# Loading both token halves of the first chunk ahead of its weights, and transposing them in one go ahead of all products

## The chip, the cores and the metric

The kernel runs on one core of a Trainium2 chip. The metric is the device time of one execution in microseconds (us). "Span" is the time from the first to the last instruction in a trace; it is about 1.9 us shorter than the device time.

## The reference

Two independent attention blocks, A and B, whose outputs are put side by side. Each projects 512 tokens of width 1024 to 32 query heads, attends to a cache with 4 key/value heads, and projects back.

```python
B, Sq, D = 16, 32, 1024              # 16*32 = 512 tokens
Hq, Hkv, Sk, Dh = 32, 4, 512, 128
q = (x @ wq).reshape(B, Sq, Hq, Dh).transpose(0, 2, 1, 3)
k, v = repeat(k_cache, 8, axis=1), repeat(v_cache, 8, axis=1)
p = softmax(einsum("bhqd,bhkd->bhqk", q, k) * Dh ** -0.5)
o = einsum("bhqk,bhkd->bhqd", p, v)
out = o.transpose(0, 2, 1, 3).reshape(B, Sq, Hq * Dh) @ wo    # bf16; for A and for B
```

## The kernel before

Only the first 8 us matter here. `x` has 1024 columns, which are 8 chunks of 128. Chunk `d` of `x`, transposed, is multiplied with chunk `d` of `wq`, and the products of the 8 chunks accumulate in PSUM, the on-chip memory that takes TensorE's results (SBUF is the one that holds its operands). The first 8 heads are computed chunk by chunk, so that TensorE can begin when the first pieces land. `TT` is 4 (128 tokens each), `NF` is 6, `HC` is 4.

```python
# loads, issued by SyncE in this order
load_x(0, 0, TT // 2)             # x columns of chunks 0 and 1, tokens 0..255, 128 KB
load_w0(0, 1, 0, NF // 2)         # weight chunk 0, heads 0..2, 96 KB
load_x(0, TT // 2, TT)            # tokens 256..511, 128 KB
load_w0(0, 1, NF // 2, NF)        # weight chunk 0, heads 3..5, 96 KB
load_w0(1, 2, 0, NF)              # weight chunk 1, heads 0..5, 192 KB
load_x(2, 0, TT)                  # chunks 2 and 3, all tokens, 256 KB
load_w0(2, 3, 0, NF)
load_w0(3, 4, 0, NF)
# ... cut: more loads

def warm_up(n):                   # products of constants, to wake TensorE's clock
    for _ in range(n):
        nc.tensor.matmul(first_q[HALF][:, 0:P], lhsT=warm, rhs=warm, start=True, stop=True)

# transpose_x(d, t0, t1, copy, ps): one TensorE transpose per 128 tokens, then one copy PSUM -> SBUF
# first_heads(heads, dcs, t0, t1): the products of these heads, chunks and tokens

warm_up(22)
for tt in range(2):
    transpose_x(0, tt, tt + 1, nc.vector.tensor_copy)
transpose_x(1, 0, 2, nc.scalar.copy, spare)
warm_up(2)
first_heads((0, 1, 2), (0,), 0, 1)
transpose_x(0, 2, TT, nc.vector.tensor_copy)
transpose_x(1, 2, TT, nc.scalar.copy)
first_heads((0, 1, 2), (0,), 1, 2)
warm_up(1)
first_heads((0, 1, 2), (0,), 2, TT)
first_heads((3, 4, 5), (0,), 0, 2)
first_heads((3, 4, 5), (0,), 2, TT)
first_heads(range(0, NF - 2), (1,))      # from here on: weight chunk 1
transpose_x(2, 0, TT, nc.vector.tensor_copy)
transpose_x(3, 0, TT, nc.scalar.copy)
first_heads(range(NF - 2, NF), (1,))
# ... cut: chunks 2 to 7, then projections, scores and values interleaved to the end
```

Of the kernel before, what the change touches and what calls it, by code (L numbers as in the profile page):

```python
# [8 lines left out]
BF16 = mybir.dt.bfloat16  # L9
# [7 lines left out]
P = 128  # L17
# [5 lines left out]
HALF = REP // 2  # L23
# [158 lines left out]
def kernel(  # L182
# [14 lines left out]
    nc = tc.nc  # L197
    B, SQ, D = A_x.shape
    SK = A_k_cache.shape[2]
    NTOK = B * SQ  # L200
    DC = D // P
    KC = SK // P
    TT = NTOK // P
# [14 lines left out]
    def fast_path(ok_i):  # L218
        with ExitStack() as fctx:
# [6 lines left out]
            psum = enter(tc.tile_pool(name="psum", bufs=2, space=bass.MemoryType.PSUM))  # L226
            enter(tc.manual_schedule())

            warm = nc.const_aps.tensor(1.0, [P, P], BF16)
# [225 lines left out]
            NF = REP - 2  # L455
# [8 lines left out]
            def load_x(d0, t0, t1):  # L464
                nc.sync.dma_start(
                    out=x_sb[:, t0:t1, d0 * P:(d0 + 2) * P],
                    in_=x_v[:, t0:t1, d0 * P:(d0 + 2) * P],
                )
# [7 lines left out]
            def load_w0(d0, d1, h0, h1):  # L476
                nc.sync.dma_start(
                    out=w0[d0 // HC][:, d0 % HC:(d1 - 1) % HC + 1, h0 * DH:h1 * DH],
                    in_=wq_v[:, d0:d1, h0 * DH:h1 * DH],
                )  # L480

            nc.scalar.preload_act_table_set("natural_log_exp_and_others")
            load_x(0, 0, TT // 2)
            load_w0(0, 1, 0, NF // 2)
            load_x(0, TT // 2, TT)
            load_w0(0, 1, NF // 2, NF)
            load_w0(1, 2, 0, NF)
            load_x(2, 0, TT)
# [18 lines left out]
            first_q = []  # L507
            for _ in range(2):
                pair_ps = psum.tile([P, 2, NW], FP32, name="q_ps", tag="s")
                first_q += [pair_ps[:, k, :] for k in range(2)]  # L510
            spare = psum.tile([P, NTOK], BF16, name="xT_ps", tag="proj")
            first_q += [psum.tile([P, NW], FP32, name="q_ps", tag="proj")[:] for _ in range(2)]

            def warm_up(n):
                for _ in range(n):
                    nc.tensor.matmul(  # L516
                        first_q[HALF][:, 0:P], lhsT=warm, rhs=warm, start=True, stop=True
                    )

            def transpose_x(d, t0, t1, copy, ps=None):  # L520
                if ps is None:
                    ps = psum.tile([P, NTOK], BF16, name="xT_ps", tag="ob")
                for tt in range(t0, t1):
                    nc.tensor.transpose(  # L524
                        ps[:, tt * P:(tt + 1) * P], x_sb[:, tt, d * P:(d + 1) * P], ident[:]
                    )
                ts = slice(t0 * P, t1 * P)
                copy(out=xT[0][:, d, ts], in_=ps[:, ts])

            def first_heads(heads, dcs, t0=0, t1=TT):  # L530
                ts = slice(t0 * P, t1 * P)
                for dc in dcs:
                    for h in heads:
                        nc.tensor.matmul(  # L534
                            first_q[h][:, ts],
                            lhsT=w0[dc // HC][:, dc % HC, h * DH:(h + 1) * DH],
                            rhs=xT[0][:, dc, ts],
                            start=(dc == 0 and t0 == 0),
                            stop=(dc == DC - 1),
                        )  # L540

            warm_up(22)
            for tt in range(2):
                transpose_x(0, tt, tt + 1, nc.vector.tensor_copy)
            transpose_x(1, 0, 2, nc.scalar.copy, spare)
            warm_up(2)
            first_heads((0, 1, 2), (0,), 0, 1)
            transpose_x(0, 2, TT, nc.vector.tensor_copy)
            transpose_x(1, 2, TT, nc.scalar.copy)
            first_heads((0, 1, 2), (0,), 1, 2)  # L550
            warm_up(1)
            first_heads((0, 1, 2), (0,), 2, TT)
            first_heads((3, 4, 5), (0,), 0, 2)
            first_heads((3, 4, 5), (0,), 2, TT)
            first_heads(range(0, NF - 2), (1,))
            transpose_x(2, 0, TT, nc.vector.tensor_copy)
            transpose_x(3, 0, TT, nc.scalar.copy)
# [68 lines left out]
            for i in range(total_slots + LAG):  # L626
                live = i < total_slots
                k, o = divmod(i, GRP)
# [52 lines left out]
    ok_i = flag.tile([1, 1], I32, name="ok_i")  # L681
    total = 2 * 2 * NG * QW
    ok = fast_path(ok_i)
    with tc.If(ok < total, preferred_fallthrough_block=True, label="general"):
        general_path(tc, problems, out_flat)
# [30 lines left out]
```

## Time and profile before

| | before |
|---|---|
| device time, median of the first 3 runs | 343.72 us (343.41 to 344.13) |
| span of the profiled run | 341.47 us |
| TensorE busy | 337.4 us, 99% of the span |
| first product of weight chunk 1 | 6.15 us |
| span minus that start | 335.32 us |

In the profile's lines, PE is TensorE, PEld its weight loads, DVE VectorE, ACT ScalarE, and SPq SyncE issuing loads. L516 is the warm-up matmul, L524 the transpose, L534 the products of the first heads, L301 the later projections. A matmul of 128x256 has 256 columns of the moving operand.

First the page of the kernel before: the span, the first line of busy time, and the chain of waits.

```profile
span 341.5 us, 5512 instructions
...
PE 337.4 (99%) x2130; PEld 214.4 (63%) x2130; DVE 265.6 (78%) x337; ACT 185.8 (54%) x209; POOL 46.7 (14%) x206
...
PE 99%; ACT 0%; issue 0%; ACTq 0%
```

TensorE bounds the kernel. But busy time covers each matmul's latency, and matmuls overlap (the page gives a 512-column one a mean of 379 ns, while they start 216 ns apart), so 99% does not prove that it runs densely. For that I compared start times. From 6.15 us to the end, 512-column matmuls start every 215 or 216 ns, and no start is late by more than 25 ns. The total is thus one number, the start of the chunk-1 products, plus a fixed train.

Next, the timeline of TensorE in the kernel before around that start. Columns: start, length, engine, line, operation, operands, shape, count.

```profile
3.24 0.63 PE L524 MATMUL xT_ps<-ident,x_sb 128*128 128x128 bf16 x4
3.67 0.42 PE L516 MATMUL q_ps<-const-bfloat16-1.0 128*128 128x128 bf16 x2
3.88 0.53 PE L534 MATMUL q_ps<-xT,w_sb 128*128 128x128 bf16 x3
4.20 0.63 PE L524 MATMUL xT_ps<-ident,x_sb 128*128 128x128 bf16 x4
4.63 0.46 PE L534 MATMUL q_ps<-xT,w_sb 128*128 128x128 bf16 x3
4.93 0.22 PE L516 MATMUL q_ps<-const-bfloat16-1.0 128*128 128x128 bf16 x1
5.00 2.19 PE L534 MATMUL q_ps<-xT,w_sb 128*128 128x256 bf16 x13
```

The last line merges the 9 remaining products of chunk 0 with the first 4 of chunk 1, as if there were no gap. The weight loads of the same stretch show the gap (the bracket is idle time of this unit and what ended it):

```profile
4.93 0.94 PEld L534 LDWEIGHTS <-w_sb 128*128 128x128 bf16 x9
6.15 0.55 PEld L534 LDWEIGHTS <-w_sb 128*128 128x128 bf16 x4 [0.28 <-DMA w_sb<-in_A_wq_dram]
```

The chain of waits of the kernel before, in order of time (start, length, what), misses it as well, because the modelled end of the matmul before it fills the hole:

```profile
5.14 1.00 PE q_ps L534 x9
6.15 0.00 issue
6.15 1.04 PE q_ps L534 x4
```

The start times say more. The last chunk-0 product starts at 5.87 and takes up 109 ns, so the next could start at 5.98. It starts at 6.15, just after weight chunk 1 landed at 6.10. Of the gap, 0.17 us is real idle time, ended by a transfer.

### The profile page before, as it was taken

The numbers are of one execution on the slowest core, as the hardware profiler recorded it, in microseconds if no ns is written. First come the engines' busy times: TensorE is split into PE (matmuls) and PEld (weight loads), VectorE is DVE, ScalarE is ACT, GpSimd is POOL, SyncE is SP. The second block draws the span as 40 slices with busy tenths as digits, with TensorE's granted clock in tenths as the row PEclk, the third lists the DMA queues.
The fourth block names the chain that finished last, engine by engine and source line by source line (L and its number), as shares of the span: only waits on it lengthen the run. The fifth ranks groups of instructions, "written<-read, shape, count | busy, mean of one in ns | idle before, by whom it ended". The sixth has DMA issues, their size and how long they took to land.

```text
span 341.5 us, 5512 instructions
## 1 busy us (share of the span) xinstructions
PE 337.4 (99%) x2130; PEld 214.4 (63%) x2130; DVE 265.6 (78%) x337; ACT 185.8 (54%) x209; POOL 46.7 (14%) x206
## 2 busy tenths in 40 slices
PE   8999999999999999999999999999999999999996
PEld 7455666666666666666666666666666666666555
DVE  1046988888988898888888988879888888889540
ACT  3058666666667667666645545555555555555110
POOL 0001110011111111110012221222122101111100
PEclk9999999999999999999999999999999999999999
DMA  6999999989996987999999955998649998440001
GB/s 194 300 192 262 295 264 196 238 244 267 277 247 154 232 232 223 192 313 263 316 272 290 280 148 142 334 270 239 117 109 291 354 186 180 98 113 6 18 18 33
DMA packets 128094, 71.70 MB, mean 210 GB/s; under 512 B 75840, under 2 KB 127296, under 8 KB 128064
## 3 DMA queue, kind: packets, MB, share of 16 engines
q1 hardware_dynamic: 127536, 70.21, 84.3%
q0 software_dynamic: 384, 1.05, 0.8%
q8 instruction: 17, 0.28, 0.3%
q14 instruction: 13, 0.11, 0.1%
q10 hardware_dynamic: 144, 0.07, 0.1%
HBM read 50.86 MB, written 2.10 MB: 155 GB/s over the span
## 4 chain that ended last, share of the span: by engine, by line
PE 99%; ACT 0%; issue 0%; ACTq 0%
PE f_ps L320 32%; PE q_ps L301 28%; PE ob L425 16%; PE s_ps L357 16%; PE q_ps L534 4%; PE q_ps L516 1%; PE xT_ps L524 0%; ACT o_sb L329 0%; ACTq L329 0%
## 5 line engine op out<-in xcount | busy, mean ns | idle before, releaser
L365 ACT ACTIVATE p_sb<-s_ps,shift 128x1024 bf16<-128x1024 f32 x128 | 142.6, 1114 | 97.7 <-PE s_ps L357 85.1
L376 DVE TRANSPOSE_TENSOR_REDUCE parts<-p_sb 128x32 f32<-128x1024 bf16 x128 | 158.7, 1240 | 20.9 <-ACT p_sb L365 19.3
L320 PE MATMUL f_ps<-wo_sb,oT 128*128 128x512 bf16 (+1 forms) x544 | 132.3, 366 | 0.0
L301 PE MATMUL q_ps<-xT,wq_sb 128*128 128x512 bf16 x448 | 116.9, 379 | 0.0
L425 PE MATMUL ob<-p_sb,v_sb 128*128 128x256 bf16 x512 | 76.8, 273 | 0.0
L357 PE MATMUL s_ps<-qT,kT 128*128 128x256 bf16 x512 | 76.8, 273 | 0.0
L320 PEld LDWEIGHTS <-oT 128*128 128x128 bf16 x544 | 53.2, 98 | 35.3
L357 PEld LDWEIGHTS <-kT 128*128 128x128 bf16 x512 | 56.9, 113 | 28.3
L301 PEld LDWEIGHTS <-wq_sb 128*128 128x128 bf16 x448 | 43.8, 98 | 32.2
L425 PEld LDWEIGHTS <-v_sb 128*128 128x128 bf16 x512 | 50.1, 98 | 20.0
L447 DVE TENSOR_TENSOR oT<-r,ob 128x512 bf16<-128x512 f32 x64 | 43.9, 686 | 20.0 <-PE ob L425 19.4
L411 DVE STREAM_TRANSPOSE r<-rall 128x512 f32<-128x512 f32 x64 | 44.2, 691 | 1.1
L309 ACT CAST qT<-q_ps 128x512 bf16<-128x512 f32 x56 | 32.6, 583 | 16.6 <-PE q_ps L301 16.6
L394 POOL COPY half<-cs 64x32 f32<-64x32 f32 x32 | 6.5, 204 | 232.1 <-DVE cs L384 232.0
L329 ACT CAST o_sb<-f_ps 128x512 bf16<-128x512 f32 (+1 forms) x17 | 9.5, 558 | 23.6 <-PE f_ps L320 23.6
L534 PE MATMUL q_ps<-xT,w_sb 128*128 128x512 bf16 (+2 forms) x73 | 14.9, 359 | 0.0
L384 DVE TENSOR_REDUCE cs<-parts 128x32 f32<-128x128 f32 x32 | 12.0, 376 | 1.1
L406 DVE RECIPROCAL rall<-sums 128x32 f32<-128x32 f32 x32 | 10.2, 319 | 3.3 <-POOL sums L403 3.3
L534 PEld LDWEIGHTS <-w_sb 128*128 128x128 bf16 x73 | 7.1, 102 | 6.8 <-DMA w_sb<-in_A_wq_dram 0.3
L566 DVE CAST qT<-q_ps 128x512 bf16<-128x512 f32 x4 | 2.5, 683 | 10.2 <-PE q_ps L534 10.2
L331 POOL DMA_DIRECT2D out_dram<-o_sb x8 | 4.6, 574 | 29.3 <-ACT o_sb L329 29.3
L395 POOL TENSOR_TENSOR half<-half,cs 64x32 f32<-64x32 f32 x32 | 7.8, 243 | 2.6
(25 smaller groups left out, 46.1 us busy)
## 6 DMA issues: line engine op xcount, KB each, us to landing
v_sb<-in_A_v_cache_dram SPq DMA_DIRECT2D x16, 512.0 KB, 5.7
wq_sb<-in_B_wq_dram SPq DMA_DIRECT2D x8, 1024.0 KB, 5.7
wo_sb<-in_A_wo_dram SPq DMA_DIRECT2D x8, 1024.0 KB, 7.1
v_sb<-in_B_v_cache_dram SPq DMA_DIRECT2D x16, 512.0 KB, 4.6
wo_sb<-in_B_wo_dram SPq DMA_DIRECT2D x8, 1024.0 KB, 8.1
wq_sb<-in_A_wq_dram SPq DMA_DIRECT2D x5, 1024.0 KB, 5.9
wq_sb<-in_A_wq_dram SPq DMA_DIRECT2D x2, 512.0 KB, 7.3
kT<-in_A_k_cache_dram SPq DMA_TRANSPOSE x64, 4.4
```

The source lines that it names most:

```text
L301: nc.tensor.matmul(ps[:], lhsT=w[:, dc, (h % 4) * DH:(h % 4 + 1) * DH], rhs=xT[pr][:, dc, :], start=(dc == 0), stop=(dc == DC - 1),)
L309: nc.scalar.copy(out=qT[pr, g][:, :, hl, :], in_=ps[:].rearrange("p (b s) -> p b s", s=SQ),)
L320: nc.tensor.matmul(ps[:, 0:width], lhsT=oT[pr, tt][:, h, :], rhs=wo_tiles[pr, nh, h // REP][:, h % REP, off:off + width], start=(h == 0), ...
L357: nc.tensor.matmul(s_ps[:, c, :], lhsT=kT[:, i % GRP, c, :], rhs=qT[pr, g][:, b, :, :].rearrange("p h s -> p (h s)"), start=True, stop=True,)
L365: nc.scalar.activation(out=p_sb[:], in_=s_ps[:], func=ACTF.Exp, bias=shift[:], scale=SCALE)
L376: nc.vector.tensor_reduce(out=parts[k][:, q, :, :].rearrange("p c h -> p (c h)"), in_=st[i]["p"][:].rearrange("p c (h s) -> p (c h) s", s=SQ),
L384: nc.vector.tensor_reduce(out=cs[:], in_=parts.pop(k)[:].rearrange("p q c h -> p q h c"), axis=AX.X, op=ALU.add,)
L406: nc.vector.reciprocal(out=rall[:, k, :], in_=quad.pop(k)[:])
L411: nc.vector.transpose(out=r[:].rearrange("p n s -> p (n s)"), in_=rall[:, k, o * 2 * REP:(o + 1) * 2 * REP] .unsqueeze(2).to_broadcast([P, ...
L425: nc.tensor.matmul(ob[j][:, q, :], lhsT=v_sb[:, i % GRP, c, :], rhs=st[i]["p"][:, c, :], start=(c == 0), stop=(c == KC - 1),)
L447: nc.vector.tensor_tensor(out=out, in0=rcp.pop(j)[:].rearrange("p (q h) s -> p q h s", h=REP), in1=ob.pop(j)[:].rearrange("p q (h s) -> p ...
L534: nc.tensor.matmul(first_q[h][:, ts], lhsT=w0[dc // HC][:, dc % HC, h * DH:(h + 1) * DH], rhs=xT[0][:, dc, ts], start=(dc == 0 and t0 == 0 ...
```

## The change

The intent was a smoother start: get both token halves of `x` on chip first, transpose all 8 blocks in a row, and then run all products of chunk 0 with no transpose between them. Three filler warm-ups go, and heads 3 to 5 run at 512 columns instead of twice 256. The second spare PSUM tile takes the buffers in which heads 4 and 5 later accumulate, so the warm-ups had to aim at head 3.

```diff
--- before.py
+++ after.py
@@ -481,8 +481,8 @@
 
             nc.scalar.preload_act_table_set("natural_log_exp_and_others")
             load_x(0, 0, TT // 2)
+            load_x(0, TT // 2, TT)
             load_w0(0, 1, 0, NF // 2)
-            load_x(0, TT // 2, TT)
             load_w0(0, 1, NF // 2, NF)
             load_w0(1, 2, 0, NF)
             load_x(2, 0, TT)
@@ -508,13 +508,13 @@
             for _ in range(2):
                 pair_ps = psum.tile([P, 2, NW], FP32, name="q_ps", tag="s")
                 first_q += [pair_ps[:, k, :] for k in range(2)]
-            spare = psum.tile([P, NTOK], BF16, name="xT_ps", tag="proj")
+            spare = [psum.tile([P, NTOK], BF16, name="xT_ps", tag="proj") for _ in range(2)]
             first_q += [psum.tile([P, NW], FP32, name="q_ps", tag="proj")[:] for _ in range(2)]
 
             def warm_up(n):
                 for _ in range(n):
                     nc.tensor.matmul(
-                        first_q[HALF][:, 0:P], lhsT=warm, rhs=warm, start=True, stop=True
+                        first_q[NF // 2][:, 0:P], lhsT=warm, rhs=warm, start=True, stop=True
                     )
 
             def transpose_x(d, t0, t1, copy, ps=None):
@@ -540,18 +540,12 @@
                         )
 
             warm_up(22)
-            for tt in range(2):
-                transpose_x(0, tt, tt + 1, nc.vector.tensor_copy)
-            transpose_x(1, 0, 2, nc.scalar.copy, spare)
-            warm_up(2)
-            first_heads((0, 1, 2), (0,), 0, 1)
-            transpose_x(0, 2, TT, nc.vector.tensor_copy)
-            transpose_x(1, 2, TT, nc.scalar.copy)
-            first_heads((0, 1, 2), (0,), 1, 2)
-            warm_up(1)
-            first_heads((0, 1, 2), (0,), 2, TT)
-            first_heads((3, 4, 5), (0,), 0, 2)
-            first_heads((3, 4, 5), (0,), 2, TT)
+            for k, ts in enumerate(((0, TT // 2), (TT // 2, TT))):
+                transpose_x(0, *ts, nc.vector.tensor_copy)
+                transpose_x(1, *ts, nc.scalar.copy, spare[k])
+            for ts in ((0, TT // 2), (TT // 2, TT)):
+                first_heads(range(0, NF // 2), (0,), *ts)
+            first_heads(range(NF // 2, NF), (0,))
             first_heads(range(0, NF - 2), (1,))
             transpose_x(2, 0, TT, nc.vector.tensor_copy)
             transpose_x(3, 0, TT, nc.scalar.copy)
```

## The prediction

> **What bounds the kernel now.** TensorE. The page gives PE 337.4 us busy of a span of 341.5, and the chain of waits is 99% PE. By the start-to-start times of the matmuls in the trace, from 6.15 us on, no start is late by more than 25 ns (one, at 7.93, waits for a VectorE copy): 512-column products start every 216 ns to the end. The total is therefore "when the products of weight chunk 1 start" plus a fixed train of about 335 us. Only what moves 6.15 pays.
>
> The first 6.15 us, from the timeline: 22 warm-ups (0.93 to 3.24, one per 107 ns), then transposes, 3 more warm-ups and the chunk-0 products without a gap, the last of them starting at 5.87. The next could start at 5.98, but starts at 6.15, released by the landing of weight chunk 1 at 6.10. The clock releases in the middle: 128-column matmuls start every 107 ns until about 4.85 us, then 512-column ones every 216. The Trainium skill, "TensorE: Matmul & The Clock Gate", section "Wait — 56ns, not 53.3ns?", gives 107/427 ns cold and 56/216 ns warm for 128/512 columns; the trace agrees (107, 216; 256 columns warm took 109).
>
> **What the change does.**
> - Loads: the second x half moves from third to second place, the first weight half from second to third. Issues are about 0.5 us apart, landings 2.2 to 2.3 us after issue: estimated x halves 3.0 and 3.5 us (was 4.04), first weights 4.0 to 4.1 (was 3.41). The second weight half (4.78), chunk 1 (6.10) and everything later have the same bytes ahead of them and the same place in the queue, so should land as before.
> - PE: removes 3 warm-ups (about 0.3 us, two cold). Eight transposes run together from 3.24 to about 4.1. Then heads 0-2 on 256 columns twice, instead of 128, 128, 256 columns: the same columns. Heads 3-5 at 512 columns: 3 matmuls instead of 6.
> - Copies: three VectorE copies become two (0.29 us each for 256 columns); two ScalarE copies (0.37 us) stay. All end in time.
>
> Estimated PE line: transposes to 4.1, heads 0-2 first half cold (3 x 213 ns) to 4.75, second half, partly warm, to 5.15, heads 3-5 (3 x 216) to 5.8. PE then waits for chunk 1, landing at 6.10.
>
> **On the critical path:** nearly nothing. About 0.2 us less PE work before 6.15 becomes idle time (0.17 to about 0.35 us) in front of the same landing. From there the same instructions run. If in some executions the clock releases later, that PE work would have passed 6.10 and removing warm-ups saves up to 0.3 us; a chunk 1 landing moved by the reorder could add or take 0.2.
>
> **Prediction:** 343.6 us, 8 in 10 within 342.9 to 344.4. Faster by over 2%: 0.005; within 2%: 0.99; slower by over 2%: 0.005.
>
> **What would show each step.** Second x half landing near 3.5 and first weights near 4.05; first product at 4.1 instead of 3.88; last chunk-0 product ending about 5.8; first chunk-1 product still at 6.1 to 6.2, released by a DMA landing; from there 216 ns spacing, and the first score matmul still near 22.6 us.
>
> **What would make it wrong.** The first weights landing well after 4.1, so PE idles and the clock release slips (each microsecond at the half clock costs about 0.5 us of products); transposes not counting as activity for the clock, so that eight in a row delay its release; chunk 1 landing earlier or later than 6.10, which moves the total one for one; an overlooked wait where heads 4 and 5 reuse the two spare transpose buffers.

## The result

| | before | after |
|---|---|---|
| device time, median | 343.88 us (343.41 to 344.16, 6 runs) | 343.44 us (343.19 to 343.82, 6 runs) |
| ratio after/before | | 0.999, interval 0.9977 to 1.0003 |
| the same, in a later session | | 0.9995, interval 0.9982 to 1.0008 |
| span of the profiled run | 341.47 us | 341.44 us |
| first product of weight chunk 1 | 6.15 us | 6.07 us |

Both intervals hold 1: no difference is resolved.

The page of the changed kernel, the same lines as shown of before:

```profile
span 341.4 us, 5454 instructions
...
PE 335.0 (98%) x2082; PEld 213.2 (62%) x2121; DVE 265.6 (78%) x336; ACT 185.8 (54%) x209; POOL 46.7 (14%) x206
...
PE 94%; DVE 1%; issue 1%; DMA 1%; SPq 1%; ACT 0%; POOL 0%; ACTq 0%
```

The fall of TensorE from 337.4 to 335.0 us is not saved work. There are 2082 matmul records beside 2121 weight loads, although the program pairs them one to one: some 40 records are missing from this trace. In the start times they show as gaps of exactly one matmul more.

The timeline of TensorE of the changed kernel, and its weight loads:

```profile
3.24 1.06 PE L524 MATMUL xT_ps<-ident,x_sb 128*128 128x128 bf16 x8
4.10 1.60 PE L534 MATMUL q_ps<-xT,w_sb 128*128 128x256 bf16 x9
6.07 1.04 PE L534 MATMUL q_ps<-xT,w_sb 128*128 128x512 bf16 x4 [0.37 <-DMA w_sb<-in_A_wq_dram]
```

```profile
4.06 1.14 PEld L534 LDWEIGHTS <-w_sb 128*128 128x128 bf16 x9
6.06 0.55 PEld L534 LDWEIGHTS <-w_sb 128*128 128x128 bf16 x4 [0.86 <-DMA w_sb<-in_A_wq_dram]
```

Eight transposes run together, nine products follow, and TensorE then stands still. The last chunk-0 product starts at 5.32 and takes up 216 ns, so chunk 0 is done at 5.54; chunk 1 begins at 6.07. The idle time grew from 0.17 to 0.53 us. Not all of this is the change's doing: as the experiments show, TensorE's clock also rose to full pace 0.52 us earlier in this execution. The chain of waits of the changed kernel now runs through the loads:

```profile
2.25 0.43 SPq L477
2.69 0.04 issue
2.73 3.29 DMA w_sb<-in_A_wq_dram
6.02 0.05 issue
6.07 1.04 PE q_ps L534 x4
```

Reading it: weight chunk 1 was issued at 2.73 and took 3.29 us to land; the products began 0.05 us later. In the kernel before it was issued at the same 2.73 and landed at 6.10. So the work that TensorE no longer does seems to have turned into waiting for the same landing. That is the theory I took into the experiments.

### The profile page after: what moved, and what is told of

It reads as the page before. It is cut to its first block, busy times and chain, and to the rows that moved or that the text cites. A ratio compares the mean times of both kernels' runs of the same rounds, so it can differ in the third digit from the quotient of the medians.

```text
span 341.4 us, 5454 instructions
## 1 busy us (share of the span) xinstructions
PE 335.0 (98%) x2082; PEld 213.2 (62%) x2121; DVE 265.6 (78%) x336; ACT 185.8 (54%) x209; POOL 46.7 (14%) x206
## 4 chain that ended last, share of the span: by engine, by line
PE 94%; DVE 1%; issue 1%; DMA 1%; SPq 1%; ACT 0%; POOL 0%; ACTq 0%
PE f_ps L320 30%; PE q_ps L301 28%; PE ob L425 17%; PE s_ps L357 16%; PE q_ps L534 4%; DMA w_sb<-in_A_wq_dram 1%; DVE parts L376 1%; ACT p_sb L365 0%; SPq L465 0%; SPq L477 0%; DVE r L411 0%; DVE oT L447 0%; PE xT_ps L524 0%; DVE cs L384 0%; ACT o_sb L329 0%
## 5 line engine op out<-in xcount | busy, mean ns | idle before, releaser
L320 PE MATMUL f_ps<-wo_sb,oT 128*128 128x512 bf16 (+1 forms) x525 | 128.2, 366 | 0.6
L301 PE MATMUL q_ps<-xT,wq_sb 128*128 128x512 bf16 x430 | 113.3, 379 | 0.5
L534 PE MATMUL q_ps<-xT,w_sb 128*128 128x512 bf16 (+1 forms) x65 | 14.2, 372 | 0.5 <-DMA w_sb<-in_A_wq_dram 0.4
L534 PEld LDWEIGHTS <-w_sb 128*128 128x128 bf16 x67 | 6.4, 99 | 7.6 <-DMA w_sb<-in_A_wq_dram 0.9
```

Source lines behind the costliest of these rows:

```text
L301: nc.tensor.matmul(ps[:], lhsT=w[:, dc, (h % 4) * DH:(h % 4 + 1) * DH], rhs=xT[pr][:, dc, :], start=(dc == 0), stop=(dc == DC - 1),)
L320: nc.tensor.matmul(ps[:, 0:width], lhsT=oT[pr, tt][:, h, :], rhs=wo_tiles[pr, nh, h // REP][:, h % REP, off:off + width], start=(h == 0), ...
L534: nc.tensor.matmul(first_q[h][:, ts], lhsT=w0[dc // HC][:, dc % HC, h * DH:(h + 1) * DH], rhs=xT[0][:, dc, ts], start=(dc == 0 and t0 == 0 ...
```

## The experiments

**Theory A:** the landing of weight chunk 1 sets the start of the dense train, and TensorE's work ahead of it has slack. **Rival B:** that work counts one for one. **Rival C:** the load order is what matters, through the landing. During the runs a refinement was needed, **theory D:** TensorE's clock, which runs at half pace at first and is then released to full pace, is released at a different time in each execution, so the slack is there in some executions and not in others. **Rival E** to D: the spread comes from elsewhere.

Start-to-start times date the release: before it, 128, 256 and 512 columns take 107, 213 and 427 ns; after it 56 (filler matmuls 58 to 60), 109 and 216 ns. The clock records in the trace give the same moments, and the table uses them (for the second run of the changed kernel, which has no record, the release is worked out from one matmul that took 304 ns). All times are in us. "Chunk 0 done" is the start of the last chunk-0 product plus its width.

| run | clock released | chunk 0 done | chunk 1 landed | chunk 1 starts | span | span minus start |
|---|---|---|---|---|---|---|
| before | 4.88 | 5.98 | 6.10 | 6.15 | 341.47 | 335.32 |
| after | 4.36 | 5.54 | 6.02 | 6.07 | 341.44 | 335.37 |
| after_again | 5.98 | 6.32 | 6.22 | 6.32 | 341.62 | 335.31 |
| order_only | 5.32 | 6.24 | 6.06 | 6.24 | 341.55 | 335.31 |
| pe_only | 5.74 | 6.41 | 6.27 | 6.41 | 341.72 | 335.31 |
| fill_8 | 6.35 | 6.94 | 6.11 | 6.94 | 342.25 | 335.30 |
| fill_40 | 3.65 | 7.74 | 6.07 | 7.74 | 343.05 | 335.30 |
| chunk1_late | 4.97 | 5.98 | 6.57 | 6.61 | 341.93 | 335.32 |
| one_issue | 4.70 | 6.66 | 5.87 | 6.66 | 342.03 | 335.37 |
| two_queues | 4.10 | 5.48 | 5.67 | 5.71 | 341.01 | 335.30 |
| two_queues_again | 5.11 | 5.97 | 6.23 | 6.28 | 341.57 | 335.30 |
| no_warm | 6.42 | 6.51 | 6.03 | 6.51 | 341.81 | 335.31 |
| anchored | 4.83 | 9.00 | 4.85 | 9.00 | 344.30 | 335.30 |
| anchored_later | 4.51 | 10.81 | 4.68 | 10.81 | 346.12 | 335.31 |

Two readings carry the rest. The last column is the same within 0.07 us in all 14 traces. And chunk 1 starts at the later of its landing (plus 0.05) and the end of chunk 0, with no third cause in any of them. All runs gave correct results.

### order_only: the new load order alone

```diff
 # the kernel before, with
 load_x(0, 0, TT // 2)
+load_x(0, TT // 2, TT)
 load_w0(0, 1, 0, NF // 2)
-load_x(0, TT // 2, TT)
 load_w0(0, 1, NF // 2, NF)
```

> The kernel before with only the new load order (second x half ahead of the first weight half); its PE program is unchanged. Theory A (the landing of weight chunk 1 sets when the dense stretch starts; what PE does ahead of it has slack): the first product now waits for the first weights, about 4.0 us instead of 3.88, chunk 0 ends by 6.0, chunk 1 still lands at 6.0 to 6.1, its first product starts at 6.05 to 6.15, the total is that of before within 0.3 us. Rival B (PE's own work ahead of chunk 1 counts one for one, and the change's small gain is its shorter PE program): also no gain here, since the PE program is the old one. Rival C (the new load order is what brought the small gain, by landing chunk 1 earlier): the total of the change, about 0.3 us under before, with chunk 1 landing near 6.02.

Measured: 343.38 us, ratio to before 0.9999 (0.9985 to 1.0013). The first product started at 4.04 and chunk 1 landed at 6.06. A's "chunk 0 ends by 6.0" failed: it ended at 6.24, after the landing, because the clock was released at 5.32 in this execution. This was the first sign that the slack is not constant. Nothing here supports C: the total did not fall, and the landings of the two orders overlap (6.02 to 6.22 in six traces of the new order, 6.06 among them; 6.10 and 6.27 in two of the old). Two traces of the old order can't rule out a shift of 0.1 us.

### pe_only: the new TensorE program alone

```diff
 # the changed kernel, with
 load_x(0, 0, TT // 2)
-load_x(0, TT // 2, TT)
 load_w0(0, 1, 0, NF // 2)
+load_x(0, TT // 2, TT)
 load_w0(0, 1, NF // 2, NF)
```

> The changed kernel with the old load order. A: the transposes of tokens 256 to 511 wait for the second x half at about 4.04, a PE gap of about 0.4 us; heads 0-2 start at about 4.5, chunk 0 ends at 5.7 to 6.0, still ahead of chunk 1 at 6.1; total as before within 0.3 us. B: the gap of 0.4 us counts, total 0.1 to 0.4 us above the changed kernel. C: the total of before, not of the change.

Measured: 343.32 us, ratio 0.9996 (0.9982 to 1.0009). The timeline of TensorE in this run shows the expected wait for the second x half:

```profile
3.24 0.63 PE L524 MATMUL xT_ps<-ident,x_sb 128*128 128x128 bf16 x4
4.09 0.61 PE L524 MATMUL xT_ps<-ident,x_sb 128*128 128x128 bf16 x4 [0.22 <-DMA x_sb<-in_A_x_dram]
4.49 2.94 PE L534 MATMUL q_ps<-xT,w_sb 128*128 128x256 bf16 x13
```

Four transposes start 0.42 us later than in the changed kernel, 4.09 instead of 3.67. In this execution the release came late (5.74), chunk 0 was done at 6.41, where A had expected 5.7 to 6.0, and the wait did count. Over five runs no difference shows. The load order is needed so that the transposes can run in one go; by itself it buys nothing measurable.

### fill_8 and fill_40: putting work into the slack

```diff
 # the changed kernel, with
+warm_up(8)          # fill_40: 40
 first_heads(range(NF // 2, NF), (0,))
```

> The changed kernel with 8 more warm-up matmuls between heads 0-2 and heads 3-5 of chunk 0 (128 columns each, 56 ns at the released clock, 0.45 us in all, less than the 0.53 us that PE idles before chunk 1). A: chunk 0 ends at about 6.0, chunk 1 starts at 6.05 to 6.15, total within 0.2 us of the changed kernel. B: total 0.45 us above the changed kernel.

> The same with 40 of them, 2.24 us. A: 0.53 us of it disappears in the wait, chunk 1 starts at about 7.75, total 1.7 us above the changed kernel. B: total 2.24 us above it. In both, PE is the releaser of nothing else and the 216 ns spacing follows.

Measured: 343.52 us (ratio 1.0002, 0.9988 to 1.0016) and 345.23 us (ratio 1.0057, 1.0043 to 1.0071).

The trace of fill_40 fits A: chunk 1 started at 7.74 against 7.75 expected, 1.67 us later than in the changed kernel, although 2.35 us of work was added. The rest vanished in the wait. Its clock had been released at 3.65, before most of this work.

The trace of fill_8 contradicted A as I had stated it. The timeline of TensorE in fill_8:

```profile
3.24 1.06 PE L524 MATMUL xT_ps<-ident,x_sb 128*128 128x128 bf16 x8
4.09 1.49 PE L534 MATMUL q_ps<-xT,w_sb 128*128 128x256 bf16 x6
5.38 1.06 PE L516 MATMUL q_ps<-const-bfloat16-1.0 128*128 128x128 bf16 x8
6.23 1.74 PE L534 MATMUL q_ps<-xT,w_sb 128*128 128x512 bf16 x7
```

The 8 fillers took from 5.38 to 6.23, 107 ns each instead of 56, since the release came at 6.35. Heads 3 to 5 began only at 6.23, and chunk 1 at 6.94. Nothing waited for a transfer. With its clock released at the same 6.35, the changed kernel would have ended chunk 0 near 6.53 (an estimate: half of each delay, as after_again shows below). So the fillers cost about 0.4 us, not the 0.85 us that they took: work done at the cold pace only pushes other work behind the release, where it runs twice as fast. The spans of its five runs were 341.5, 341.6, 341.7, 342.2 and 342.5: in three of them most of the filling was hidden, in two it was not.

The times of fill_40 alone would speak for B. Dividing its ratio by that of the changed kernel (0.999 and 0.9995) gives 2.1 to 2.3 us above the changed kernel, where A expected 1.7 and B 2.24. But its five spans are 343.0, 343.1, 343.3, 344.1 and 344.3. The first three are 1.4 to 1.9 us above the seven shortest of the changed kernel (341.4 to 341.6), the last two 2.1 to 2.5 above its four longest (341.8 to 342.0). That would be slack in the one group and B's full price in the other; but four of these five executions have no trace, and the pairing is assumed. The traces separate the theories where the times do not: the same kernel has slack when the release is early, and none when it is late.

### chunk1_late: moving the landing

```diff
 # the changed kernel, with
-load_w0(1, 2, 0, NF)
 load_x(2, 0, TT)
+load_w0(1, 2, 0, NF)
```

> The changed kernel with the 256 KB x load of chunks 2 and 3 issued ahead of weight chunk 1. A: chunk 1 lands about where that x load landed before, 6.8 instead of 6.02, its first product starts at about 6.85, and the total rises by 0.7 to 0.9 us over the changed kernel, one for one with the landing. B (PE's own work sets it): total unchanged within 0.2 us.

Measured: 343.83 us, ratio 1.0011 (0.9998 to 1.0024). The landing came at 6.57, not 6.8, so the expected size was too large by 0.2 us. The chain of waits of this run shows the landing in command:

```profile
3.20 3.36 DMA w_sb<-in_A_wq_dram
6.57 0.05 issue
6.61 1.04 PE q_ps L534 x4
```

TensorE was done with chunk 0 at 5.98 and waited 0.63 us. Against the changed kernel, the landing moved by 0.55 us, the start by 0.54 and the span by 0.49. In a trace with an early release the landing counts one for one. All five spans are 341.9 us or more, as a start at 6.61 and a train of 335.3 us demand. This speaks for A and against B.

### one_issue and two_queues: an earlier landing?

```diff
 # one_issue: the changed kernel, with
-load_w0(0, 1, 0, NF // 2)
-load_w0(0, 1, NF // 2, NF)
+load_w0(0, 1, 0, NF)
```

```diff
 # two_queues: the changed kernel, with these two issued by ScalarE, ahead of its table load
-load_x(0, TT // 2, TT)
+load_x(0, TT // 2, TT, nc.scalar)
-load_w0(0, 1, NF // 2, NF)
+load_w0(0, 1, NF // 2, NF, nc.scalar)
```

> The changed kernel with the two weight halves of chunk 0 in one load, so that every later load is issued one slot (0.47 us) earlier. If the pace of issuing limits the early supply (96 to 128 KB per 0.47 to 0.51 us slot is 190 to 270 GB/s, below the 370 GB/s that the trace shows from 5.5 us on), chunk 1 lands at 5.5 to 5.7 instead of 6.02; the first product waits for the whole 192 KB, at 4.2 to 4.5; chunk 0 ends at 5.6 to 5.9; by A the total falls 0.2 to 0.4 us below the changed kernel. If the transfer itself limits, chunk 1 lands at 6.0 as before and the total stays. B: the total rises by the later first product, 0.1 to 0.4 us.

> The changed kernel with the second x half and the second weight half issued by ScalarE ahead of its table load, so that SyncE issues chunk 1 two slots (1.0 us) earlier. A with the issue pace as limit: chunk 1 lands at 5.0 to 5.5, before PE is through with chunk 0 at about 5.5; PE then goes on without a wait and the total falls by about 0.5 us below the changed kernel. A with the transfer as limit: chunk 1 lands near 5.8 to 6.0, total falls by 0.2 us at most. B: no change.

> The kernel of two_queues once more, to settle whether it beats both. D: where the release comes early its span is 341.0 to 341.1 (the landing at 5.67 instead of 6.05), where it comes late it is PE-bound like the changed kernel; mean 0.1 to 0.2 us below the changed kernel, spread larger. If it were a true gain of the whole 0.35 us, the lowest and the mean would both fall by that.

Measured: one_issue 343.75 us (ratio 1.0004, 0.9991 to 1.0017); two_queues 343.54 (1.0003, 0.9990 to 1.0016) and, run again, 343.52 (1.0002, 0.9989 to 1.0015).

In one_issue the joined weights took much longer than I had worked out. The chain of waits of that run:

```profile
1.75 3.55 DMA w_sb<-in_A_wq_dram
5.30 0.04 issue
5.35 2.34 PE q_ps L533 x13
```

They landed at 5.30 instead of 4.2 to 4.5, while in the changed kernel both halves had landed by 4.83. TensorE idled from 4.10 to 5.35, and chunk 1, although its weights were there at 5.87, began at 6.66. The 3.55 us are nothing special: chunk 1, also 192 KB, took 3.0 to 4.5 us in the 14 traces. Why one load of 192 KB takes longer here than two of 96 KB stays open.

In two_queues chunk 1 was issued 0.98 us earlier, at 1.75. It landed at 5.67 in one trace and at 6.23 in the other:

```profile
1.75 4.48 DMA w_sb<-in_A_wq_dram
6.23 0.05 issue
6.28 1.04 PE q_ps L534 x4
```

These last lines are the chain of two_queues_again. So an earlier issue was partly or wholly eaten by a longer transfer. The Trainium skill ("DMA: Bandwidth & Descriptors", section "Issuing engines are not separate DMA queues") says that issuing from several engines only saves the sequencer's time, as all transfers share the same 16 DMA engines; these two traces agree. The expected 0.5 us did not appear in the times, nor did the 0.1 to 0.2 us expected of the repeat. One run of ten reached a span of 341.0, below anything else measured, but no version here is shown to beat both kernels.

### no_warm: the clock

```diff
 # the changed kernel, with
-warm_up(22)
```

> The changed kernel without its 22 first warm-ups. PE starts at the transposes, about 3.1 us, and the clock is released about 3.5 to 4 us of work later, at 6.5 to 7.5 instead of 4.45. Chunk 0 then takes its cold time (0.85 us of transposes, six times 213 ns, three times 427 ns) and ends at about 6.5, and chunk 1 and part of chunk 2 run at 427 ns: total 1 to 2 us above the changed kernel. If the warm-ups did nothing: total unchanged.

Measured: 343.93 us, ratio 1.0021 (1.0005 to 1.0036), spans from 341.7 to 343.1. TensorE first worked at 3.09 and the clock was released at 6.42. Chunk 0 was done at 6.51, long after the landing at 6.03. By the ratio the mean rose by 0.7 us over before. Against the changed kernel, to which the expected 1 to 2 us refer, that is 0.9 to 1.1 us (its ratio divided by 0.9995 or 0.999): the low end. Warm-ups do pay, and a late release makes the landing irrelevant.

### after_again, anchored and anchored_later: is the spread the clock's?

```diff
 # anchored: the changed kernel, with all x loads moved behind weight chunk 3, and
-warm_up(22)
+warm_up(64)
 # anchored_later: moved behind two more weight loads of 256 KB each, and warm_up(76)
```

> The changed kernel once more, for its spread and a second trace. New theory D (from the traces so far): the clock is released at a different time in every execution, 3.7 to 6.3 us in ten traces, and the total is 335.3 us plus the later of two things: the landing of chunk 1 (about 6.05) and the end of PE's chunk-0 work, which moves by half of every delay of the release. Then the trace shows span minus start of the first chunk-1 product = 335.3 within 0.1 again, and that product starts at 6.07 if the release is before about 5.4 us, else later (up to 6.7). Spans of the runs between 341.3 and 342.1 as before. Rival E: the spread of 0.7 us comes from elsewhere (loads, the 335 us train), and the difference stays at 335.3 in no fixed way.

> The changed kernel with the x loads issued after the weights of chunks 0 to 3, and 64 warm-ups instead of 22, so that x lands at about 7.5 to 8.5 us and the clock is released in every execution before PE has real work. D: all chunk-0 work runs at the released clock (transposes 56 ns, 256 columns 109 ns), chunk 1 starts about 1.8 us after the x landing, at 9.3 to 10.3, total 3.3 to 4.2 us above the changed kernel, and the spread of the spans shrinks from 0.6 to 0.8 us to 0.3 us or less (what is left is the landing). E: the total rises as much, but the spread stays 0.6 us or more.

> The run called anchored was not clean: x landed at 6.9 us, before 64 warm-ups at the cold pace end (7.75), so a late release still moved PE's start. Here two more 512 KB and 256 KB weight loads go ahead of x, estimated landing 8.2 to 8.7, and 76 warm-ups, which end before that for any release up to about 7 us (56 cold, 20 released: 0.93 + 6.0 + 1.2 = 8.1). D: everything after the x landing runs at the released clock in every execution, the total is 346.8 to 348 us, and the spans agree within 0.4 us (landing only). E: they spread by 0.6 us or more, as those of the kernel before do (341.4 to 342.2).

The second trace of the changed kernel is the best pair to the first, as the program is the same. The timeline of TensorE and the chain of waits of after_again:

```profile
3.24 1.06 PE L524 MATMUL xT_ps<-ident,x_sb 128*128 128x128 bf16 x8
4.10 3.25 PE L534 MATMUL q_ps<-xT,w_sb 128*128 128x256 bf16 x13
```

```profile
3.45 0.85 PE xT_ps L524 x8
4.30 3.05 PE q_ps L534 x13
```

Everything up to 4.10 is as in the first trace. Then the products run at the cold pace until about 5.98, chunk 0 is done at 6.32 instead of 5.54, and the 13 products of both chunks run through without the wait for the landing at 6.22. The release came 1.62 us later and chunk 0 ended 0.78 us later, about half of it, as it must when the cold pace is half the released one. Its five spans were 341.4 to 341.8, and span minus start was 335.31. That is D as expected.

(The sizes of the two loads in the last expectation are mistaken; both are 256 KB.)

anchored (346.06 us, ratio 1.0075) was not a clean test: x landed at 6.91, earlier than planned, and 64 warm-ups at the cold pace last to 7.75. Its spans still spread from 343.9 to 345.2. The corrected anchored_later (348.29 us, ratio 1.0154) gave spans of 346.1, 346.2, 346.4, 346.6 and 348.4. Four agree within 0.5 us, the fifth is 2 us out with a lower mean granted clock (0.995 against 1.0). The expectation "within 0.4 us" was missed. TensorE idled for 1.6 us before x landed in the trace of that kernel, so the clock may have been taken back in the fifth run. Its mean clock fits: 0.995 over 348.4 us is 1.7 us of lost clock, an estimate of some 3.5 us at half pace. But that run has no trace. This test of D is inconclusive; what carries D is the table of 14 traces.

## Why the prediction was right

**What bounds the kernel.** Right. The train of 335.3 us after the start of chunk 1 held in all 14 traces, within 0.07 us, for every load order and every amount of work ahead of it.

**The loads.** Right. Predicted: second x half near 3.5, first weights 4.0 to 4.1, second weight half 4.78 and chunk 1 at 6.10 as before. Measured in the changed kernel: 3.46, 4.02, 4.83 and 6.02. The first score matmul started at 22.52, with 22.6 predicted. With the same bytes ahead of it and the same place in the queue, chunk 1 landed at 6.02 to 6.27 in eight traces of different kernels, with the old order at 6.10 and 6.27.

**TensorE's work.** Right in its starts: 8 transposes from 3.24, the first product at 4.10 against 4.1 predicted. Chunk 0 ended at 5.54 instead of 5.8. The miss is the clock: released at 4.36 in this execution, 4.88 in the one I had read. Half of that 0.52 us is the 0.26 us of the miss.

**The critical path.** Right for the profiled execution: the removed work became idle time in front of the landing. But only about 0.2 us of the growth from 0.17 to 0.53 us is that work, as predicted. The rest is luck of the execution: about 0.25 us came from the earlier release, and 0.08 us went because chunk 1 landed earlier. What was mis-sized is how often this holds. The prediction took the release of the trace, "about 4.85 us", as the rule and a later one as a side case in "some executions". In the traces with the 22 warm-ups it lies anywhere from 3.65 to 6.35 us (6.42 without them). Of 40 executions of the kernel before with a recorded span, 27 lie at 341.3 to 341.7 and 13 at 341.9 to 342.2; of 11 of the changed kernel, 9 lie at 341.4 to 341.8 and 2 at 341.9 and 342.0. That is what one would see if the late releases lost some work and the early ones did not. Spans of 341.9 to 342.2 mean a start of chunk 1 at 6.6 to 6.9, later than any landing traced with the load in this place of the queue (6.02 to 6.27), so a late landing is no likely rival.

The mean granted clock of each execution gives a second sign. It is below 1.000 in 10 of the 13 late executions of before and in none of the 27 early ones. The record of no_warm shows how such a value arises: released at 6.42, the clock was taken back at 340.92, 98 windows of 3413 ns later and before the end of the span, so such a value suggests a late release; the ten other traces with a clock record and x loaded first, released at 6.35 or earlier, read 1.000. (A value of 1.000 proves nothing, as after_again has no clock record at all.) The changed kernel has 3 such executions: 341.8, 341.8 and 341.9, against 342.0 to 342.2 in those 10. That is some 0.25 us less in executions with a late release, near the 0.2 us of removed work. But three executions are few, none of the thirteen has a trace, and the comparison was made after the fact.

**The total.** Predicted 343.6 (342.9 to 344.4), measured 343.44. The range is 1.5 us wide and would have held whether or not the removed work paid, so the number alone confirms little. An estimate of the gain: at an equal release the shorter program ends chunk 0 about 0.2 us earlier (5.98 in before, 5.78 by the measured paces with the release at 4.88; not the 0.3 us that the prediction gave the warm-ups). Counting in the third of executions that are late, that is 0.07 us, or 0.02%. The intervals are about 0.13% to either side and cannot show it. So the gain is not shown; the clock values above speak for it, no more.

## What to carry to other kernels

When one engine runs densely to the end, find the moment at which the dense train starts and ask which arrival sets it: only that moves the total. Work removed ahead of a later arrival turns into idle time, and the next arrival to look at may be a clock, not a transfer. One trace is one draw of a clock that is released at a different time in each execution, so read several before you call a slack fixed, and count the records before you believe that busy time fell.

## What the Trainium skill lacked or had wrong

- "TensorE: Matmul & The Clock Gate", section "What's actually happening", says that the activity window is 3413 ns long, runs freely and does not restart with the kernel. These traces agree: the released stretch of the kernel before lasts 337.92 us in the clock records, 99 windows of 3413 ns, and the release moved from 3.65 to 6.35 us although the first matmul always came at 0.93. But its section "What you observe" puts the release around 4 us into the activity, give or take 0.5. Here it came 2.72 us after the first matmul in fill_40 (3.65) and 5.42 us after it in fill_8 (6.35), a much wider range.
- The same page, section "Wait — 56ns, not 53.3ns?": its gaps of 107, 427, 56 and 216 ns were met (106 to 107, 427, 55 to 57, 215 to 216), but the fillers of fill_40 started every 58 to 60 ns at the released clock.
- The same page, "Part 4: PE-mode transpose", says that the full clock does not engage for transposes. Here they start every 107 ns before the release and every 56 ns after it, like other matmuls. Whether transposes count as activity that brings the release on, no run here tests.
- The same page counts the cost of the ramp as under 1% of a kernel. That holds here: from the first matmul at 0.93 to the release are 2.7 to 5.4 us in the traces with 22 warm-ups, and half of that, an estimate of what it costs, is under 1% of 341 us. Beyond saying that the ramp varies from run to run, and advising to warm up first, the page has no word on what it means for a comparison of two kernels: the spans of before differ by 0.9 us, more than the effect of this change.
- "DMA: Bandwidth & Descriptors" has nothing on why one 192 KB load took 3.55 us early in the kernel, while two of 96 KB, issued at 1.75 and 2.25, were both there by 4.83.
- No page says that the profile's row of granted clock does not show the cold start: it reads 9 from the first slice on, in the kernel before, although the clock was released only at 4.88. The first clock record begins at the release, and the time before it counts as full.
